# Gated recurrence and ELU MLP on one core: the weights' range check moved to ScalarE and GpSimd, and the schedule of the units rewritten

## Chip, core and metric

The kernel runs on one core of a Trainium2 chip. The metric is the device time of one execution in microseconds (us). TensorE is called PE in the profile, VectorE DVE, ScalarE ACT, GpSimd POOL and SyncE SP.

## What is computed

Attention first: for each batch and head a complex state S of 48 x 48 decays by a per-step, per-channel factor whose magnitude is capped at 0.999, and takes in the outer product of k and v; the output is q times the real part of S. Then an MLP on all 3072 tokens, in float32, with weights that arrive as float64.

```
mag = sqrt(a_re*a_re + a_im*a_im);  scale = minimum(mag, 0.999) / (mag + 1e-6)
for t in range(768):                       # B=4, H=8, D=48
    S_re, S_im = ar*S_re - ai*S_im + k_t v_t^T,  ar*S_im + ai*S_re
    y[t] = q_t . S_re
x = y as (3072, 384)
h = x @ w_in                               # 384 x 2048
g = where(h > 0, h, exp(min(h, 0)) - 1)    # ELU
out = g @ w_out                            # 2048 x 384
```

## The kernel before

The work is cut into 12 **units**: a unit `u` is 128 tokens of two batches (`NB`), all heads. For each unit the kernel makes, in this order:

- *decays*: `squares`, `logarithms`, `noted` (minimum and maximum for a final check that picks a general kernel where the inputs are out of range), `angles` (arc tangent) and `carried` (adds the angle of the unit before on one row). Squares, logarithms and exponentials are ScalarE's (L604 to L618), the products with them GpSimd's (L606, L619, L620; VectorE's for unit 0, by `products`), and two steps are VectorE's: L621, which ends the tangent's argument, and L626, which caps the logarithm.
- *gates*: `turns` (TensorE L664 sums the angles over tokens, VectorE takes the fraction), `waves` (sine and cosine), `decays` (L686, L691), `gated` (q and k times decay and wave: L717, L719, VectorE for q, GpSimd for k).
- *values*, for each batch n: `transposed` q and k (L739, copies L740), `scores` (L747, mask L752), `states` (L768; the state S is added on VectorE, L779, and decayed on GpSimd, L780), `values` (L790, L797, copies L805, L809). `seam` moves some rows of x by DMA from GpSimd (L819).
- *hidden layer*, eight steps `hidden`: six matmul instructions each (L831, twelve records, since a float32 matmul leaves two), then the ELU: ScalarE L836 and L837, VectorE L838 into the tile g.
- *output layer*, eight steps `project`, four instructions each (L847), four steps for each of two blocks of 128 tokens; the result is copied by ScalarE (L853) and stored from SP (L855).

`hidden` and `project` share three PSUM tiles (tag "mlp"), everything else on TensorE shares three (tag "w").

**The weights** come as 14 parts, six of `w_in` (1024 columns) and eight of `w_out` (768 columns), fetched by SP as pairs of 32-bit words (`fetch`) and turned into float32 by `rounded`, seven VectorE operations each, L567 to L585: five build the value from exponent, mantissa and the low word, and the last two (L582, L585) put a value of too small an exponent to zero. `fetches(n)` fetches the next n parts, `converts(n)` issues the next n operations.

**The order** is written out by hand and no scheduler changes it: `plan` is a list of slots, 16 for a unit, each a list of calls, and each engine executes its instructions in the order in which the calls issue them. In the steady part, for unit u, in slots of its own period: `hidden` at 4 to 11, its `project` at 28 to 35, one period later; the gates of unit u + 1 at 0 to 3 and its values from 6; the decays of unit u + 2 at 8 to 12 (`early`). Unit 0 runs ahead of the loop, by itself.

Of the kernel before, what the change touches and what calls it, by code (L numbers as in the profile page):

```python
# [436 lines left out]
def kernel(  # L437
# [94 lines left out]
    def weights_of(kind, m):  # L532

        if kind == "in":
            i, f = m % NI, m // NI * WC
            dst = w_in[:, i, f : f + WC]
            t = sb.tile([C, WC, 2], U32, tag="g", bufs=4, name="w64")
# [20 lines left out]
    def rounded(kind, m):  # L558

        w, dst = raw.pop((kind, m))
# [5 lines left out]
            out=p, in0=hi, scalar1=LOW, scalar2=3, op0=ALU.bitwise_and,  # L568
# [3 lines left out]
            out=f, in0=hi, scalar=TOP, in1=p, op0=ALU.bitwise_and, op1=ALU.bitwise_or  # L572
        )
        yield nc.vector.tensor_scalar(
# [18 lines left out]
    def products(u):  # L593

        return nc.vector if u == 0 else nc.gpsimd
# [12 lines left out]
    def logarithms(u):  # L608
# [11 lines left out]
        products(u).tensor_tensor(out=x0, in0=ai, in1=x0, op=ALU.mult)  # L620
        nc.vector.scalar_tensor_tensor(  # L621
            out=flat(x0), in0=flat(lr), scalar=-2.0, in1=flat(x0), op0=ALU.add, op1=ALU.mult
        )
        x["t"] = x0
        x["l"] = new("n", 6)
        nc.vector.scalar_tensor_tensor(  # L626
            out=flat(x["l"]), in0=flat(lm), scalar=2 * float(np.log(CAP)), in1=flat(e),
            op0=ALU.min, op1=ALU.subtract,
        )

# [271 lines left out]
    SLOTS = 16  # L902

    def recurrence(first, base, n_only=None):
        at = [[0, 1, 2, 3, 5], [3, 4, 6, 7, 8]]
        fns = [
            [
                lambda u, n=n: transposed(u, "q", n), lambda u, n=n: transposed(u, "k", n),
                lambda u, n=n: scores(u, n), lambda u, n=n: states(u, n),
                lambda u, n=n: values(u, n),  # L910
            ]
            for n in range(NB)
        ]
# [3 lines left out]
    def decaying(*at):
        return list(zip(at, (squares, logarithms, noted, angles, carried)))

    def gating(*at):  # L920
        return list(zip(at, (turns, waves, decays, gated)))

    once = recurrence(decaying(0, 1, 1, 3, 3) + gating(4, 5, 5, 6), 7)
    steady = recurrence(gating(0, 1, 2, 3), 6)
    early = decaying(8, 9, 9, 12, 12)


    plan = [[] for _ in range((NU + 3) * SLOTS)]

    def put(at, fn, u):  # L930
        plan[at].append(lambda: fn(u))

    for u in range(1, NU):
        for at, fn in once if u < 3 else steady:
            put((u - 1) * SLOTS + at, fn, u)
        if u > 2:
            for at, fn in early:
                put((u - 2) * SLOTS + at + 2 * (u == 3), fn, u)
# [73 lines left out]
```

## Time and profile before

| | us |
|---|---|
| median of 3 executions | 859.19 (857.25 to 861.69) |
| the profiled execution | 860.39 |
| its span in the profile | 858.6 |
| PE, matmuls: busy | 721.1 (84%) |
| PE, weight loads: busy | 529.8 (62%) |
| VectorE, ScalarE, GpSimd: busy | 327.6, 388.2, 235.3 |

A busy share is a mean over a start, in which the weights are converted, and a steady part, in which unit follows unit; each is to be read from its own stretch. PEclk is the granted clock of TensorE as a share of 2.4 GHz. A row of the timeline has the start in us, the duration in us, and in brackets how long the engine was idle before it and what ended that. Instructions behind one another on an engine may overlap a little, so that a sum of durations is slightly above the time they take.

### The profile page before, as it was taken

Reading aid. Unit: us, or ns where it says so; the run is one execution under the profiler, and the core shown is the slowest. Engines: PE = TensorE matmul, PEld = TensorE weight load, DVE = VectorE, ACT = ScalarE, POOL = GpSimd, SP = SyncE. Lnnn points to the kernel's source line nnn. Section 1 sums busy time; section 2 is a strip of 40 time slices with the busy share of each in tenths; the row PEclk is TensorE's granted clock in tenths of the full one; section 3 lists DMA queues with packets and bytes.
Section 4 is the critical chain, followed back from the end, with each engine's and each line's share of the span. In section 5 each row is a group of like instructions: output and inputs, shape, how many; then the busy total and the mean of one; then the engine's idle time right before and its main releaser. Section 6 shows DMA issues by size and latency. Waiting matters only on the chain.

```text
span 858.6 us, 12795 instructions
## 1 busy us (share of the span) xinstructions
PE 721.1 (84%) x5346; PEld 529.8 (62%) x5346; DVE 327.6 (38%) x401; ACT 388.2 (45%) x591; POOL 235.3 (27%) x210
## 2 busy tenths in 40 slices
PE   1436283559978998999999999999999989999997
PEld 0325072437667686686686686685785776776853
DVE  4973999861323234223323223323323232320200
ACT  5315432544467446346365463472572573431400
POOL 0131132231443242342432523422432421401000
PEclk9667586778989999999999999999999999999999
DMA  9993325501230322122122212302403300000000
GB/s 171 149 170 60 74 52 147 120 1 39 51 66 10 61 47 37 35 47 37 33 48 37 55 26 40 72 7 43 75 2 67 50 2 15 11 1 24 1 21 21
DMA packets 136075, 43.48 MB, mean 51 GB/s; under 512 B 128536, under 2 KB 133192, under 8 KB 135240
## 3 DMA queue, kind: packets, MB, share of 16 engines
q1 hardware_dynamic: 132160, 41.14, 25.5%
q0 software_dynamic: 3776, 1.36, 1.4%
q8 instruction: 44, 0.72, 0.4%
q14 instruction: 23, 0.19, 0.1%
q10 hardware_dynamic: 72, 0.07, 0.0%
HBM read 36.55 MB, written 4.79 MB: 48 GB/s over the span
## 4 chain that ended last, share of the span: by engine, by line
PE 58%; issue 16%; DVE 10%; POOL 8%; ACT 4%; DMA 2%; SPq 1%; DVEq 0%; POOLq 0%; ACTq 0%
PE mlp L847 29%; PE mlp L831 18%; PE w L739 3%; PE w L768 2%; POOL n L619 2%; POOL n L620 2%; DMA w<-in_moe_w_in_dram 2%; PE y L797 2%; PE w L747 2%; PE w L664 1%; DVE g L838 1%; DVE least L634 1%; POOL S L780 1%; DVE most L637 1%; PE w L686 1%
## 5 line engine op out<-in xcount | busy, mean ns | idle before, releaser
L831 PE MATMUL mlp<-x,w_in 128*128 128x256 f32 x1152 | 273.8, 392 | 23.3 <-DMA x<-y 23.2
L847 PE MATMUL mlp<-w_out,g 128*128 128x384 f32 x768 | 271.3, 507 | 16.9 <-DVE g L838 16.9
L831 PEld LDWEIGHTS mlp<-x,w_in 128*128 128x128 f32 x1152 | 221.7, 197 | 58.1 <-issue 25.0
L847 PEld LDWEIGHTS mlp<-w_out,g 128*128 128x128 f32 x768 | 148.6, 197 | 117.8 <-DVE g L838 18.0
L838 DVE SCALAR_TENSOR_TENSOR g<-ee,mlp 128x512 f32<-128x512 f32 x96 | 65.0, 685 | 214.6 <-ACT ee L837 211.7
L836 ACT ACTIVATE ee<-mlp 128x512 f32<-128x512 f32 x96 | 57.1, 595 | 157.0 <-PE mlp L831 124.6
L780 POOL TENSOR_TENSOR S<-S,T 96x384 f32<-96x384 f32 x40 | 35.5, 888 | 206.8 <-DVE S L779 206.8
L853 ACT COPY o<-mlp 128x384 f32<-128x384 f32 x24 | 11.5, 479 | 130.5 <-PE mlp L847 124.5
L739 PE MATMUL w<-ident,qg 128*96 128x128 f32 x192 | 31.0, 303 | 42.0 <-DVE qg L719 36.5
L837 ACT ACTIVATE ee<-ee 128x512 f32<-128x512 f32 x96 | 60.5, 630 | 3.0
L739 PEld LDWEIGHTS w<-ident,qg 128*96 128x96 f32 x192 | 22.5, 138 | 49.0 <-DVE qg L719 39.1
L719 POOL TENSOR_TENSOR kg<-k,cs 128x1536 f32<-128x1536 f32 x11 | 51.9, 4718 | 0.9
L805 ACT COPY x<-y 128x384 f32<-128x384 f32 x24 | 11.3, 473 | 89.5 <-PE y L797 89.5
L740 ACT COPY qt<-w 96x512 f32<-96x512 f32 x48 | 26.8, 579 | 45.2 <-PE w L739 45.0
L621 DVE SCALAR_TENSOR_TENSOR n<-n 128x768 f32<-128x768 f32 x12 | 11.5, 958 | 91.4 <-POOL n L620 91.4
L664 PE MATMUL w<-n,sum_turns 128*128 128x384 f32 x48 | 21.8, 586 | 27.0 <-ACT n L647 21.0
L717 POOL TENSOR_TENSOR k<-k,n 128x768 f32<-128x768 f32 x11 | 23.9, 2171 | 71.7 <-ACT n L691 71.7
L819 POOL DMA_DIRECT2D x<-y x72 | 35.5, 500 | 26.7 <-ACT y L809 26.7
L669 DVE TENSOR_SCALAR rnd<-w 128x384 f32<-128x384 f32 x24 | 13.4, 557 | 73.7 <-PE w L664 72.4
L606 POOL TENSOR_TENSOR n<-n 128x768 f32<-128x768 f32 x11 | 19.9, 1810 | 77.9 <-ACT n L605 77.9
L768 PEld LDWEIGHTS w<-vn,kg 64*96 64x96 f32 x704 | 34.5, 161 | 9.5 <-issue 9.3
L619 POOL TENSOR_TENSOR n<-ar,n 128x768 f32<-128x768 f32 x11 | 20.1, 1824 | 63.8 <-ACT n L617 63.8
(72 smaller groups left out, 791.9 us busy)
## 6 DMA issues: line engine op xcount, KB each, us to landing
w<-in_moe_w_out_dram SPq DMA_DIRECT2D x8, 768.0 KB
ar<-in_a_re_dram SPq DMA_DIRECT2D x24, 192.0 KB, 3.0
ai<-in_a_im_dram SPq DMA_DIRECT2D x24, 192.0 KB, 4.5
w<-in_moe_w_in_dram SPq DMA_DIRECT2D x12, 384.0 KB, 14.3
q<-in_q_dram SPq DMA_DIRECT2D x24, 192.0 KB, 3.5
k<-in_k_dram SPq DMA_DIRECT2D x24, 192.0 KB, 4.8
vn<-in_v_dram SPq DMA_DIRECT2D x24, 192.0 KB, 3.4
out_dram<-o SPq DMA_DIRECT2D x24, 192.0 KB, 2.0
```

Source lines behind the costliest of these rows:

```text
L619: products(u).tensor_tensor(out=lr, in0=ar, in1=x0, op=ALU.mult)
L664: nc.tensor.matmul(t, lhsT=sum_turns, rhs=x["th"][:, n].rearrange("p h d -> p (h d)"), start=True, stop=True,)
L719: eng.tensor_tensor(out=o, in0=g.rearrange("p n h d -> p (n h) d").unsqueeze(2).to_broadcast(shape), in1=x["cs"], op=ALU.mult,)
L739: nc.tensor.transpose(t[:, h], x[key + "g"][:, n, h0 + h], ident)
L768: nc.tensor.matmul(g[:, h], lhsT=x["kg"][ts(c, L), n, h], rhs=vn[u % 2][ts(c, L), n, h, 0:D], start=True, stop=True,)
L780: nc.gpsimd.tensor_tensor(out=new_s, in0=new_s, in1=wide, op=ALU.mult)
L819: nc.gpsimd.dma_start(out=x["x"][ds(j * HP + D, G), i], in_=x["y"][ds(j * HP + i * G, G)])
L831: nc.tensor.matmul(t[:, e], lhsT=w_in[:, i, ts(f + e, C)], rhs=x["x"][:, i], start=(i == 0), stop=(i == NI - 1),)
L836: nc.scalar.activation(out=e, in_=t, func=AF.Relu, scale=-1.0)
L837: nc.scalar.activation(out=e, in_=e, func=AF.Exp, scale=-1.0)
L838: nc.vector.scalar_tensor_tensor(out=x["g", f // 8][:, f % 8 : f % 8 + 2], in0=e, scalar=-1.0, in1=t, op0=ALU.add, op1=ALU.max)
L847: nc.tensor.matmul(x["o"], lhsT=x["g", f // 8][:, f % 8, ts(n, C)], rhs=w_out[:, f], start=(f == 0), stop=(f == NF - 1),)
```

## The change

Four things change. In `rounded`, the two last operations on VectorE go: the high words are squared by ScalarE as float32 (in place), GpSimd compares the square with 2^-30 and multiplies the converted weights in place; the buffer of the fetched words is now read by GpSimd last. `slopes` holds the two VectorE steps that stood in `logarithms`, and is called later. `products` gives VectorE the products of units 0 and 1. And the plan is written anew: the output layer of a unit follows its hidden layer, decays start three slots later, units 0 and 1 run interleaved ahead of the first hidden layer, thirty matmuls on the identity (`warm`) stand ahead of unit 0's transposes, and fetches and conversions have their own tables.

```diff
     def rounded(kind, m):
         yield nc.vector.tensor_scalar(
-            out=p, in0=hi, scalar1=LOW, scalar2=3, op0=ALU.bitwise_and,
+            out=f, in0=hi, scalar1=LOW, scalar2=3, op0=ALU.bitwise_and,
             op1=ALU.logical_shift_left,
         )
...
+        size = hi.bitcast(FP32)
+        nc.scalar.activation(out=size, in_=size, func=AF.Square)
...
-        yield nc.vector.tensor_tensor(out=p, in0=p, in1=f, op=ALU.add)
-        yield nc.vector.tensor_scalar(
-            out=hi, in0=hi, scalar1=EXP, scalar2=None, op0=ALU.bitwise_and
-        )
-        yield nc.vector.scalar_tensor_tensor(
-            out=dst, in0=hi, scalar=float(LEAST), in1=p, op0=ALU.is_ge, op1=ALU.mult
-        )
+        yield nc.vector.tensor_tensor(out=dst, in0=p, in1=f, op=ALU.add)
+        yield nc.gpsimd.tensor_scalar(
+            out=size, in0=size, scalar1=LEAST_SQ, scalar2=None, op0=ALU.is_ge
+        )
+        nc.gpsimd.tensor_tensor(out=dst, in0=dst, in1=size, op=ALU.mult)
...
-        return nc.vector if u == 0 else nc.gpsimd
+        return nc.vector if u < 2 else nc.gpsimd
...
+    def slopes(u):
         nc.vector.scalar_tensor_tensor(
-            out=flat(x0), in0=flat(lr), scalar=-2.0, in1=flat(x0), op0=ALU.add, op1=ALU.mult
+            out=flat(t), in0=flat(w), scalar=-2.0, in1=flat(t), op0=ALU.add, op1=ALU.mult
...
+    def warm(n):
+        t = ps.tile([C, C], FP32, tag="mlp", bufs=3, name="mlp")
+        for _ in range(n):
+            nc.tensor.matmul(t, lhsT=ident, rhs=ident, start=True, stop=True)
...
+    FETCHES = [(-32, 1), (-29, 1), (-27, 1), (-26, 1), (-18, 1), (-12, 1), (-10, 2), (-1.5, 1), (0.5, 1)]
+    FETCHES += [(3.5, 1), (5.5, 1), (7.5, 1), (9.5, 1)]
+    CONVERTS = [(-28, 2), (-26, 2), (-25, 2), (-24, 1)] + [(-20 + i, 1) for i in range(12)]
+    CONVERTS += [(-8 + i, 3) for i in range(22)]
...
+    decays_of(0, -30, -29, -28, -27, -28, -28)
+    gates_of(0, -26, -25, -25, -23)
+    put(-24, warm, 30)
+    values_of(0, -20)
+    decays_of(1, -22, -21, -18.5, -8, -18, -18)
+    gates_of(1, -17, -16, -15.5, -12.5)
+    values_of(1, -10)
+    layer_of(0, 4, 20)
+    layer_of(1, 12, 28)
+    for u in range(2, NU):
+        r = (u - 2) * SLOTS
...
+        decays_of(u, r + 11, r + 12, r + 14, r + 14, r + 15, r + 15)
+        gates_of(u, r + 16, r + 17, r + 18, r + 19)
+        values_of(u, r + 22)
+        layer_of(u, r + 36, r + 44)
```

In it `decays_of` takes the slots of squares, logarithms, slopes, noted, angles and carried, `gates_of` those of turns, waves, decays and gated, `values_of` the first slot of the values, and `layer_of` the first slot of the hidden and of the output layer. `(-8, 3)` in CONVERTS stands for three operations in slot -8.

**VectorE, one steady unit.** Before (g is the ELU's output, a the masked scores, S the state, n the decay tiles, ar and ai the factors):

```order
L838 SCALAR_TENSOR_TENSOR g<-ee,mlp 128x512 x4
L752 TENSOR_TENSOR a<-w,mask 128x512
L838 SCALAR_TENSOR_TENSOR g<-ee,mlp 128x512
L779 TENSOR_TENSOR S<-w,S 96x384 x2
L621 SCALAR_TENSOR_TENSOR n<-n 128x768
L626 SCALAR_TENSOR_TENSOR n<-n 128x768
L634 TENSOR_REDUCE least<-ar 128x1
L637 TENSOR_REDUCE most<-ai 128x1
L838 SCALAR_TENSOR_TENSOR g<-ee,mlp 128x512 x3
L752 TENSOR_TENSOR a<-w,mask 128x512
L653 SCALAR_TENSOR_TENSOR n<-carry,n 1x768
L779 TENSOR_TENSOR S<-w,S 96x384 x2
```

Now:

```order
L845 SCALAR_TENSOR_TENSOR g<-ee,mlp 128x512 x5
L759 TENSOR_TENSOR a<-w,mask 128x512
L845 SCALAR_TENSOR_TENSOR g<-ee,mlp 128x512
L786 TENSOR_TENSOR S<-w,S 96x384 x2
L845 SCALAR_TENSOR_TENSOR g<-ee,mlp 128x512 x2
L759 TENSOR_TENSOR a<-w,mask 128x512
L786 TENSOR_TENSOR S<-w,S 96x384 x2
L629 SCALAR_TENSOR_TENSOR n<-n 128x768
L632 SCALAR_TENSOR_TENSOR n<-n 128x768
L641 TENSOR_REDUCE least<-ar 128x1
L644 TENSOR_REDUCE most<-ai 128x1
L660 SCALAR_TENSOR_TENSOR n<-carry,n 1x768
```

The four decay operations moved from ahead of the last three ELU steps to behind all eight and behind both state sums.

**ScalarE, the end of the same unit's hidden layer.** Before (the last rows of the ELU, then the arc tangent with its table, then the copies of y and of the output tile o):

```order
L837 ACTIVATE ee<-ee 128x512
L647 ACT_TABLE_LOAD
L647 ACTIVATE n<-n 128x768
L805 COPY x<-y 128x2x3x64
L809 COPY y<-y 128x128
L853 COPY o<-mlp 128x384
```

Now:

```order
L620 ACT_TABLE_LOAD
L620 ACTIVATE n<-n 128x768
L621 ACTIVATE n<-n,ln_eps 128x768
L812 COPY x<-y 128x2x3x64
L816 COPY y<-y 128x128
L860 COPY o<-mlp 128x384
L654 ACT_TABLE_LOAD
L654 ACTIVATE n<-n 128x768
```

The arc tangent stands behind the copy of o now, and the logarithms and exponentials (L620, L621) stand right ahead of the copies of y.

**VectorE, the first ELU steps of unit 0.** Before, between operations of the weights (w, wp, wf, w_in):

```order
L578 SCALAR_TENSOR_TENSOR wp<-w_127,wp 128x1024
L838 SCALAR_TENSOR_TENSOR g<-ee,mlp 128x512
L581 TENSOR_TENSOR wp<-wp,wf 128x1024
L582 TENSOR_SCALAR w_127<-w_127 128x1024
L585 SCALAR_TENSOR_TENSOR w_in<-w_127,wp 128x1024
```

Now:

```order
L583 SCALAR_TENSOR_TENSOR wp<-w_758,wp 128x768
L586 TENSOR_TENSOR w_out<-wp,wf 128x768
L570 TENSOR_SCALAR wf<-w_782 128x768
L845 SCALAR_TENSOR_TENSOR g<-ee,mlp 128x512
L574 SCALAR_TENSOR_TENSOR wf<-w_782,wf 128x768
L579 TENSOR_SCALAR wp<-wf 128x768
L583 SCALAR_TENSOR_TENSOR wp<-w_782,wp 128x768
L845 SCALAR_TENSOR_TENSOR g<-ee,mlp 128x512
L586 TENSOR_TENSOR w_out<-wp,wf 128x768
```

The first ELU step stood in the fourth weight part and stands in the tenth now; the last addition of the weights stands between the second and the third ELU step of unit 1. On GpSimd each part's compare and multiply (L587, L590) follow the order of the parts, and those of the last two stand around the products of unit 2's decays.

## Rows read from the trace of the kernel before

**Rows 1.** Windows: start and end, length, busy (instructions) of PE, PEld, DVE, ACT, POOL; PEclk, DMA, GB/s.

```profile
0.00:34.30 34.30, 5.12 (x8) 2.15 (x8) 20.59 (x23) 17.51 (x20) 3.17 (x11) 0.86 1.00 160
34.30:57.60 23.30, 14.70 (x256) 12.78 (x256) 22.71 (x25) 7.24 (x14) 7.56 (x10) 0.72 1.13 164
```

**Rows 2.** Windows: one unit of the steady part.

```profile
428.58:490.13 61.55, 58.97 (x458) 43.37 (x457) 19.57 (x25) 31.89 (x49) 21.07 (x19) 0.97 0.22 41
```

**Rows 3.** Timeline of all engines in that unit, around the last ELU steps.

```profile
457.24 0.96 DVE L621 SCALAR_TENSOR_TENSOR n<-n 128x768 f32<-128x768 f32 x1 [8.70 <-POOL n L620]
...
460.70 1.27 DVE L838 SCALAR_TENSOR_TENSOR g<-ee,mlp 128x512 f32<-128x512 f32 x2
...
461.44 4.51 PE L847 MATMUL mlp<-w_out,g 128*128 128x384 f32 x8 [2.11 <-DVE g L838]
```

**Rows 4.** Windows: behind a short stop, and behind the 2.11 us stop.

```profile
123.40:124.10 0.70, 0.01 (x1) 0.00 (x0) 0.70 (x3) 0.00 (x0) 0.00 (x0) 1.00 0.00 0
124.10:124.90 0.80, 0.64 (x4) 0.39 (x4) 0.80 (x3) 0.05 (x1) 0.00 (x0) 1.00 0.00 0
...
461.40:463.00 1.60, 1.56 (x3) 0.96 (x4) 0.81 (x2) 1.48 (x3) 0.00 (x0) 0.50 1.09 216
```

**Rows 5.** Timeline of VectorE: the two kinds of weight operations, at both widths.

```profile
94.78 0.69 DVE L567 TENSOR_SCALAR wp<-w 128x1024 uint32<-128x1024 uint32 x1
95.50 1.23 DVE L571 SCALAR_TENSOR_TENSOR wf<-w,wp 128x1024 uint32<-128x1024 uint32 x1
...
134.58 0.55 DVE L567 TENSOR_SCALAR wp<-w 128x768 uint32<-128x768 uint32 x1
135.16 0.96 DVE L571 SCALAR_TENSOR_TENSOR wf<-w,wp 128x768 uint32<-128x768 uint32 x1
```

**Rows 6.** Groups by line and shape: busy us, mean ns | idle before.

```profile
L847 PE MATMUL mlp<-w_out,g 128*128 128x384 f32 x768 | 271.3, 507 | 16.9 <-DVE g L838 16.9
L838 DVE SCALAR_TENSOR_TENSOR g<-ee,mlp 128x512 f32<-128x512 f32 x96 | 65.0, 685 | 214.6 <-ACT ee L837 211.7 <-PE w L686 3.0
...
L606 POOL TENSOR_TENSOR n<-n 128x768 f32<-128x768 f32 x11 | 19.9, 1810 | 77.9 <-ACT n L605 77.9
...
L604 ACT ACTIVATE n<-ar 128x768 f32<-128x768 f32 x12 | 10.0, 835 | 0.0
...
L882 POOL MEMSET vn<- 128x256 f32 x2 | 0.6, 311 | 0.0
```

**Rows 7.** Timeline of all engines: a weight operation beside GpSimd's product.

```profile
107.10 4.85 POOL L719 TENSOR_TENSOR kg<-k,cs 128x1536 f32<-128x1536 f32 x1
108.56 4.21 DVE L571 SCALAR_TENSOR_TENSOR wf<-w,wp 128x768 uint32<-128x768 uint32 x1
```

**Rows 8.** Timeline of the steady unit: decay chain and TensorE's groups.

```profile
449.67 0.84 ACT L614 ACTIVATE n<-n 128x768 f32<-128x768 f32 x1
...
455.39 1.81 POOL L620 TENSOR_TENSOR n<-ai,n 128x768 f32<-128x768 f32 x1
...
462.75 1.28 ACT L647 ACT_TABLE_LOAD   x1
...
464.92 0.94 DVE L653 SCALAR_TENSOR_TENSOR n<-carry,n 1x768 f32<-1x768 f32 x1 [0.87 <-ACT n L647]
465.88 1.44 PEld L768 LDWEIGHTS w<-vn,kg 64*96 64x96 f32 x32 [0.55 <-issue]
...
467.37 2.85 PE L847 MATMUL mlp<-w_out,g 128*128 128x384 f32 x8
...
470.15 0.69 PE L790 MATMUL y<-a,vn 64*64 64x64 f32 x32
...
471.80 1.56 PE L847 MATMUL mlp<-w_out,g 128*128 128x384 f32 x4
```

**Rows 9.** Chain that ended last, its end: start us, us, what.

```profile
789.91 20.72 PE mlp L831 x96
...
823.65 28.59 PE mlp L847 x88
```

More of the change, by code (lines that the diff above doesn't have):

```diff
@@ L917, in decaying @@
[L917 to L938, printed above, removed]
@@ new lines, with put, decays_of @@
+    FETCHES = [(-32, 1), (-29, 1), (-27, 1), (-26, 1), (-18, 1), (-12, 1), (-10, 2), (-1.5, 1), (0.5, 1)]
+    FETCHES += [(3.5, 1), (5.5, 1), (7.5, 1), (9.5, 1)]
+    CONVERTS = [(-28, 2), (-26, 2), (-25, 2), (-24, 1)] + [(-20 + i, 1) for i in range(12)]
+    CONVERTS += [(-8 + i, 3) for i in range(22)]
+    SLOTS = 16
+    plan = []
+    def put(at, fn, *args):
+        plan.append((at, len(plan), lambda: fn(*args)))
+    def decays_of(u, *at):
+        for x, fn in zip(at, (squares, logarithms, slopes, noted, angles, carried)):
+            put(x, fn, u)
@@ new lines, in gates_of, with values_of, layer_of @@
+    def gates_of(u, *at):
+        for x, fn in zip(at, (turns, waves, decays, gated)):
+            put(x, fn, u)
+    def values_of(u, base):
+        for n, at in enumerate([[0, 1, 2, 3, 5], [3, 4, 6, 7, 8]]):
+            for x, (fn, *args) in zip(at, (
+                (transposed, u, "q", n), (transposed, u, "k", n), (scores, u, n),
+                (states, u, n), (values, u, n),
+            )):
+                put(base + x, fn, *args)
+        put(base + 9, seam, u)
+    def layer_of(u, at_h, at_p):
+        for m in range(NF // 2):
+            put(at_h + m, hidden, u, 2 * m)
@@ L948 @@
         for m in range(NF // 2):
             n, q4 = divmod(m, NF // 4)
-            put(
-                (u + 1) * SLOTS + (9 if u == 0 else 12) + m,
-                lambda u, n=n, q4=q4: project(u, n, 4 * q4, 4 * q4 + 4), u,
-            )
-    fetches(1)
-    load_qk(0)
-    fetches(1)
-    load_v(0)
-    fetches(1)
-    load_a(1)
-    fetches(1)
-    between = {angles: 3, decays: 4, gated: 4}
-    for at, fn in once:
-        fn(0)
-        if fn is gated:
-            load_qk(1)
-        converts(between.get(fn, int(at >= 7)))
@@ L968 @@
-    load_v(1)
-    for at, fns in enumerate(plan):
-        if at < 2 * SLOTS:
-            fetches(1 if at < 8 else at % 2)
-            converts(3 if at < 8 else 4 if at < SLOTS else 3)
-        for fn in fns:
-            fn()
-        if at == NU * SLOTS:
-            verdict()
+            put(at_p + m, project, u, n, 4 * q4, 4 * q4 + 4)
+    for at, fn, u in (
+        (-31, load_qk, 0), (-30, load_v, 0), (-28, load_a, 1), (-21, load_qk, 1), (-20, load_v, 1),
+    ):
+        put(at, fn, u)
@@ L977 @@
+    for at, n in FETCHES:
+        put(at, fetches, n)
+    for at, n in CONVERTS:
+        put(at, converts, n)
+    put(NU * SLOTS, verdict)
+    for _, _, do in sorted(plan, key=lambda x: x[:2]):
+        do()
     ctx.close()
```

44 lines of the change are left out of this document (15 added, 29 removed).

## The prediction

> **What bounds the kernel now.** I read the stretches of the span first, then the chain of waits, then the timeline of one unit of work on all engines. In the steady part one unit takes 61.55 us, of which TensorE is busy 58.97 [rows 2]. So TensorE sets the time there, and only its stops can be won. The reader finds one such stop in each unit: VectorE starts a decay step at 457.24 after 8.70 us of waiting for GpSimd, the ELU steps (L838) queued behind it start only at 460.70, and TensorE, whose PSUM tile for the next output group they free, waits 2.11 us [rows 3]. That wait costs more than itself: right behind it the granted clock is 0.50 (1.2 GHz) where it was 1.00 (2.4 GHz) before; behind a stop of 0.7 us, from 123.40 to 124.10, it stayed at 1.00 [rows 4]. The eight matmuls that began at 461.44 took 4.51 us including the slow stretch [rows 3], where eight at full clock move on in 2.78 (467.37 to 470.15 [rows 8]). That is 1.7 us, and with the remainder of the slow stretch I take 1.84. So a stop is worth 2.11 + 1.84 = 3.95 us, and a unit without it takes 61.55 - 3.95 = 57.6 us.
>
> Ahead of the steady part the bound is another one. VectorE is busy 20.59 of the first 34.3 us and 22.71 of the next 23.3 [rows 1]: it converts the weights, and nothing of the MLP can run without them.
>
> **The change, part by part.**
>
> *Decay steps behind the ELU steps.* The 3.95 us stop goes. The trace has it in eight units (TensorE's matmuls of L847 wait 16.9 us in all for L838 [rows 6], eight times 2.11), which makes -31.6 us. But the whole decay chain now starts three slots later, and two things become late. I count from the end of a unit's last hidden matmul.
>
> First, GpSimd's queue holds the two products of the decays (L619, L620 before, L622, L623 now) ahead of the state product S. S must wait for: the y matmuls 1.65 us (470.15 to 471.80 [rows 8]), ScalarE's two copies of them, an estimated 0.7 from their 384 and 128 columns at the squares' rate, two squares and GpSimd's add, 2 x 0.835 + 1.81 = 3.5 [rows 6], logarithms and products 7.53 (449.67 to 457.20 [rows 8]), and S's own multiply, 0.9 at 384 columns: some 14.3 us. TensorE arrives where it needs S after 1.65 + 2.78 + 1.1 + 2.78 + 1.49 + 2.78 + 0.6 = 13.2 us: output-layer groups as from 467.37 to 470.15, the state matmuls 465.88 to 467.37 [rows 8], a part of the y matmuls, an estimated 0.6 of the 1.65, and for the scores an estimate of 1.1 from these like groups of 32 small matmuls. So a wait of about 1.1 us.
>
> Second, the arc tangent now stands on ScalarE behind the copy of the output tile, which ends only when TensorE has finished the first token half. The copy of 384 columns, an estimated 0.5 at the squares' rate [rows 6], then table load, arc tangent and VectorE's carry step (462.75 to 465.86, 3.1 us [rows 8]) make 3.7 us with gaps; TensorE has one group of eight matmuls, 2.6 us, to do before it needs the angles. Again about 1.1 us. Neither wait is in the trace of before; their bounds are 0 (the chains run a little faster than I add up) and 2.11 each with the clock's fall. I take 1.1 without a fall, because they are nearer to the 0.7 us stop that left the clock at 1.00 than to the 2.11 us one [rows 4]. Nine units have late decays: 9 x 2.15 = +19.4 us. The net of this part is -12.2 us.
>
> *Output layer right behind the first.* It moves 64 matmul records of each unit one unit earlier and adds or removes none: 0 us, as long as their cover holds. What they covered was TensorE's time under gates and values; the new neighbours there are the same unit's matmuls, so the cover stays.
>
> *Weights' range check.* VectorE loses two operations in each of 14 weight parts: 0.69 + 1.23 us in six parts of 1024 columns, 0.55 + 0.96 in eight of 768 [rows 5], in all 23.6 us. ScalarE gets a square each (0.84 us at 768 columns [rows 6]), which hides beside VectorE's next operations. GpSimd gets a multiply, 1.81 us at 768 columns [rows 6] and so 2.41 at 1024, and a compare that the trace does not show. Its bounds are GpSimd's memset, 311 ns for 256 columns [rows 6], hence 0.93 and 1.24 us, and the multiply's own price. I take the lower, as the compare reads one operand and not two. That is 6 x 3.65 + 8 x 2.74 = 44 us on GpSimd (58 at the upper bound). The Trainium skill, GPSIMD Engine Reference, section 4.1, calls one-input work on this engine roughly line rate; 1024 columns would be an estimated 0.85 us, and the sum some 3 us lower.
>
> Is GpSimd's 44 us beside VectorE's work? The rows say mostly not. VectorE's L571, 0.96 us alone [rows 5], took 4.21 us when it met GpSimd's product of 4.85 us and ended 0.8 us after it [rows 7]: operations with two SBUF inputs waited it out. VectorE's operations on PSUM (L838, the masks, the states) and its own waits leave room; they are about a third of its time in this stretch. So I put two thirds, 29 us, on VectorE's path; bounds 0 and 44.
>
> *First units reordered, unit 1's products on VectorE, fetches.* I add up VectorE's queue up to the last addition of the weights, which now stands between the second and third ELU of the second unit. The first 57.6 us hold 43.30 us of VectorE work [rows 1], of which three weight parts of seven operations (3 x 6.99) and 5.0 of a fourth; so unit 0's own work is 17.4, and unit 1's the same, because its products are now VectorE's. Weights: five operations stay, 2 x 0.69 + 3 x 1.23 = 5.07 and 2 x 0.55 + 3 x 0.96 = 3.98 [rows 5], together 62.3. Ten ELU steps at 0.685 [rows 6]: 6.9. Work: 34.8 + 62.3 + 6.9 = 104. Waits: 57.6 - 43.3 = 14.3 in the first unit with the 7.8 us start; for unit 1, whose logarithms stand uncovered, 3.9 (the 7.53 of [rows 8] less two products of 1.81) and, an estimate, as much again for its sines, together 8. With GpSimd's 29 the last addition ends near 104 + 22.3 + 29 = 155 us. Then the four decay operations (457.24 to 460.70, 3.5 us [rows 3]), a carry step of 0.94 [rows 8] and two hidden steps of 20.72 / 8 us [rows 9] pass until the second unit's hidden layer ends: **165 us**.
>
> What queues behind the new waits: on SP, the fetch of a weight part now waits for GpSimd's multiply of the part whose buffer it takes, and behind it stand the loads of unit 2; these are needed some 30 us later, so I cost them at nothing. If that cover went, one late load of two tensors, 786 KB at 160 GB/s [rows 1], would cost 5 us.
>
> *Filler matmuls.* Thirty of 128 columns, sixty records of half a hidden matmul's columns: 20.72 / 96 / 2 = 0.11 us each at full clock, twice that at half, so 6.5 to 13 us. They stand between decays and transposes of unit 0, where TensorE has some 10 us free. Cost 0 to 3, gain 0 to 3 (faster transposes, whose copies wait for ScalarE's logarithms anyway): 0.
>
> **The sum.** From 165 us on TensorE does ten units at 57.6 = 576, the output layers of units 0 and 1 at 28.59 x 64 / 88 = 20.8 each [rows 9] = 41.6, the new waits 19.4, and the tail behind the last matmul, 858.6 - 852.2 = 6.4 [rows 9]: 643.4. The span becomes 808, the execution 808 + 1.8 = 810 against 860.39; that execution stands 1.2 us above the median of 859.19, so the forecast is **809 us**.
>
> **The rivals.**
> 1. *GpSimd's checks run free beside VectorE.* For it: many of VectorE's steps in that stretch read PSUM. Against: rows 7. Then 29 us go: 780.
> 2. *They exclude each other wholly.* For it: the 4.21 us row. Against: the room just named. All 44 us on the path: 824. The Trainium skill, Advanced Engine Details and Errata, section VectorE Performance Modes, says that GpSimd instructions and two-port VectorE instructions block each other; by that rule, taken for every operation here, this is the case, and the row of 4.21 us agrees.
> 3. *The two new waits let the clock fall* as the 2.11 us one did: 18 x 1.84 = +33 us: 842. For it: the fall at 461.40; against: none behind 0.7 us.
> 4. *The new waits aren't there*, because ScalarE and GpSimd run a little ahead of my count: 790.
> 5. *Slower than before.* GpSimd's compare is the price: the 14 compares stand in VectorE's way one by one, and each microsecond more costs 14. The forecast has 50 us to lose, so it decides at some 3.6 us more than I took, a compare near 5 us, twice GpSimd's two-operand rate. At 6 us: 809 + 14 x 4.7 = 875. Against: no row of GpSimd is so slow per column.
> 6. *The change doesn't do what it says*, and the ELU steps still wait for GpSimd: 809 + 31.6 = 841.
>
> **How the numbers follow.** The forecast has 0.40; rivals 1 and 2 0.18 and 0.13; 3 and 6 0.12 and 0.02; 4 0.07; 5 0.08, of which 0.02 within the bound that follows. The range runs from 776 (rival 1 with the cheaper end of the small costs) to 842 (rival 3). About 0.5% is what a measurement of this kernel can tell from no change. Faster: 0.92; the same: 0.02; slower: 0.06.
>
> **What would show it.** Right: the decay step L629 (L621 before) starts behind the last ELU step, and TensorE's wait for the ELU steps is gone; a steady unit near 59.7 us; the hidden layer of the second unit ending near 165 us; VectorE operations stretched where GpSimd's multiply or compare runs. Wrong: a steady unit of 57.6 (rival 4) or 63 (rival 3); hidden layers ending near 136 (rival 1) or 180 (rival 2); GpSimd busy without pause up to 200 us (rival 5).

## The result and the profile after

The changed kernel takes **831.63 us** (median of 4 runs, 829.47 to 831.91) against 858.22 us (854.53 to 861.69) for the kernel before, run beside it: ratio 0.9685, 95% interval 0.964 to 0.973. The profiled span is 829.6 us, its mean granted clock 0.952. The forecast was 809 us in a range of 776 to 842: the direction and the range held, and of the 50 us forecast 27 came.

Windows of the changed kernel, columns as in [rows 1]: up to the end of the last weight addition, from there to the end of unit 1's hidden layer, and one steady unit:

```profile
0.00:165.20 165.20, 90.43 (x736) 73.10 (x737) 132.82 (x123) 79.61 (x109) 94.83 (x60) 0.78 0.63 116
165.20:184.75 19.55, 14.69 (x54) 11.19 (x53) 10.32 (x13) 11.12 (x14) 2.41 (x2) 0.83 0.42 61
247.52:307.53 60.01, 57.67 (x457) 42.54 (x456) 19.76 (x26) 32.21 (x49) 22.50 (x19) 1.00 0.25 42
```

Its steady unit is 60.01 us where the forecast had 59.7 and [rows 2] 61.55. From 184.75 us to the end it takes 644.85 us, forecast 643.4. So all that is missing was lost ahead of 184.75 us, which the forecast had put at 165. Of the 29.0 us between the two profiled spans (858.6 and 829.6), nine steady units account for some 14 (1.54 us each); the rest was won outside them, and no run takes apart which piece of the new order won it. TensorE's timeline of the steady unit, the only rows there with a wait of half a microsecond or more, shows what it lost:

```profile
289.57 0.99 PE L804 MATMUL y<-qt,S 96*48 96x64 f32 x28 [0.65 <-POOL S L787]
...
297.13 1.53 PE L671 MATMUL w<-n,sum_turns 128*128 128x384 f32 x4 [1.21 <-DVE n L660]
```

The stop for the ELU in [rows 3] is gone, and on VectorE the first decay step stands behind the last ELU step:

```profile
276.82 0.69 DVE L845 SCALAR_TENSOR_TENSOR g<-ee,mlp 128x512 f32<-128x512 f32 x1 [2.78 <-ACT ee L844]
...
290.03 0.94 DVE L629 SCALAR_TENSOR_TENSOR n<-n 128x768 f32<-128x768 f32 x1
```

The two forecast waits, for the state product and for the carry step, are there, at 0.65 and 1.21 us, and the granted clock of the unit is 1.00 throughout: no fall behind either.

The groups of the weight conversion in the changed kernel, VectorE's for parts of 768 and 1024 columns (L570, L574, L579, L583, L586; [rows 5] has 0.55 and 0.96, 0.69 and 1.23 us for the two kinds), then ScalarE's square (L578), GpSimd's compare (L587) and multiply (L590):

```profile
L574 DVE SCALAR_TENSOR_TENSOR wf<-w,wf 128x768 uint32<-128x768 uint32 x8 | 14.1, 1766 | 0.1
L574 DVE SCALAR_TENSOR_TENSOR wf<-w,wf 128x1024 uint32<-128x1024 uint32 x6 | 11.2, 1870 | 0.1
...
L570 DVE TENSOR_SCALAR wf<-w 128x768 uint32<-128x768 uint32 x8 | 8.4, 1055 | 0.3
...
L587 POOL TENSOR_SCALAR w<-w 128x768 f32<-128x768 f32 x8 | 20.3, 2539 | 6.2 <-ACT w L578 5.7
L587 POOL TENSOR_SCALAR w<-w 128x1024 f32<-128x1024 f32 x6 | 20.0, 3338 | 0.6
...
L590 POOL TENSOR_TENSOR w_out<-w_out,w 128x768 f32<-128x768 f32 x8 | 16.7, 2094 | 1.9 <-DVE w_out L586 1.6
L590 POOL TENSOR_TENSOR w_in<-w_in,w 128x1024 f32<-128x1024 f32 x6 | 15.4, 2575 | 0.5
...
L578 ACT ACTIVATE w<-w 128x768 f32<-128x768 f32 x8 | 7.4, 920 | 34.1 <-DVE wf L574 34.1
```

GpSimd spends 72.4 us on the check, not 44: the compare, 2.54 and 3.34 us, is dearer than the multiply with its two operands. VectorE's L574 takes 1.8 and 1.5 times its own time. And in the eight parts of 768 columns the square waits 34.1 us for VectorE, with ELU operations behind it on ScalarE.

The section on the change leaves one thing out: the buffers are shared in another way. In the kernel before, the fetched `w_out` parts had a tag of their own. Now half of them have the tag `g1`, which the ELU's tiles of odd units use too, and GpSimd's multiply is the last to read a fetched part. So VectorE's first ELU step of unit 1 waits for GpSimd and starts as the multiply ends (157.45):

```profile
153.13 2.41 POOL L587 TENSOR_SCALAR w<-w 128x768 f32<-128x768 f32 x1
...
155.62 1.83 POOL L590 TENSOR_TENSOR w_out<-w_out,w 128x768 f32<-128x768 f32 x1
...
157.48 0.69 DVE L845 SCALAR_TENSOR_TENSOR g<-ee,mlp 128x512 f32<-128x512 f32 x1 [4.02 <-POOL w_out L590]
```

VectorE is idle from 153.46 on, so the first two rows also show GpSimd's two operations with next to nothing beside them.

Two theories could explain the 20 us lost in the start. **A:** GpSimd's operations stretch VectorE's, and that is the price. **B:** the square, waiting in ScalarE's queue ahead of the ELU, makes TensorE wait. Beside both stands a third possibility, that the forecast of the start was wrong without any check.

### The profile page after: what moved, and what is told of

Its sections match the earlier page's. It is cut to its first block, busy times and chain, and to the rows that moved or that the text cites. A ratio compares the mean times of both kernels' runs of the same rounds, so it can differ in the third digit from the quotient of the medians.

```text
span 829.6 us, 12975 instructions
## 1 busy us (share of the span) xinstructions
PE 720.4 (87%) x5406; PEld 532.3 (64%) x5406; DVE 336.2 (41%) x378; ACT 403.0 (49%) x604; POOL 307.4 (37%) x233
## 4 chain that ended last, share of the span: by engine, by line
PE 49%; issue 18%; DVE 12%; ACT 8%; POOL 7%; DMA 3%; SPq 2%; POOLq 0%; ACTq 0%; DVEq 0%
PE mlp L838 21%; PE mlp L854 17%; PE w L746 3%; POOL S L787 3%; PE w L671 2%; DVE wf L574 2%; POOL n L623 2%; POOL n L622 2%; DMA w<-in_moe_w_out_dram 2%; PE w L754 2%; DMA w<-in_moe_w_in_dram 2%; SPq L509 1%; PE w L693 1%; ACT L654 1%; DVE wp L583 1%
## 5 line engine op out<-in xcount | busy, mean ns | idle before, releaser
L838 PE MATMUL mlp<-x,w_in 128*128 128x256 f32 x1152 | 268.0, 388 | 24.3 <-DVE g L845 24.3
L854 PE MATMUL mlp<-w_out,g 128*128 128x384 f32 x768 | 262.9, 492 | 0.0
L854 PEld LDWEIGHTS mlp<-w_out,g 128*128 128x128 f32 x768 | 142.2, 190 | 92.0
L787 POOL TENSOR_TENSOR S<-S,T 96x384 f32<-96x384 f32 x40 | 48.2, 1206 | 191.2 <-DVE S L786 191.2
L786 DVE TENSOR_TENSOR S<-w,S 96x384 f32<-96x384 f32 x40 | 22.1, 552 | 77.0 <-PE w L775 39.2
L726 POOL TENSOR_TENSOR kg<-k,cs 128x1536 f32<-128x1536 f32 x10 | 47.1, 4713 | 0.8
L775 PEld LDWEIGHTS w<-vn,kg 64*96 64x96 f32 x704 | 37.1, 171 | 12.0 <-issue 9.0
L747 ACT COPY qt<-w 96x512 f32<-96x512 f32 x48 | 26.4, 577 | 35.9 <-PE w L746 35.7
L587 POOL TENSOR_SCALAR w<-w 128x768 f32<-128x768 f32 (+1 forms) x14 | 40.3, 2881 | 6.7 <-ACT w L578 5.7
L775 PE MATMUL w<-vn,kg 64*96 64x48 f32 x704 | 40.3, 257 | 2.5 <-ACT n L698 1.7
L578 ACT ACTIVATE w<-w 128x768 f32<-128x768 f32 (+1 forms) x14 | 14.3, 1019 | 51.9 <-DVE wf L574 38.5
```

Of the source, the lines that this page charges most:

```text
L587: yield nc.gpsimd.tensor_scalar(out=size, in0=size, scalar1=LEAST_SQ, scalar2=None, op0=ALU.is_ge)
L726: eng.tensor_tensor(out=o, in0=g.rearrange("p n h d -> p (n h) d").unsqueeze(2).to_broadcast(shape), in1=x["cs"], op=ALU.mult,)
L747: nc.scalar.copy(out=o[:, h0 : h0 + 4], in_=t)
L775: nc.tensor.matmul(g[:, h], lhsT=x["kg"][ts(c, L), n, h], rhs=vn[u % 2][ts(c, L), n, h, 0:D], start=True, stop=True,)
L787: nc.gpsimd.tensor_tensor(out=new_s, in0=new_s, in1=wide, op=ALU.mult)
L838: nc.tensor.matmul(t[:, e], lhsT=w_in[:, i, ts(f + e, C)], rhs=x["x"][:, i], start=(i == 0), stop=(i == NI - 1),)
```

## Experiments on the range check

**The check back on VectorE.** The rest of the change as it is:

```diff
-        nc.scalar.activation(out=size, in_=size, func=AF.Square)
...
-        yield nc.vector.tensor_tensor(out=dst, in0=p, in1=f, op=ALU.add)
-        yield nc.gpsimd.tensor_scalar(
-            out=size, in0=size, scalar1=LEAST_SQ, scalar2=None, op0=ALU.is_ge
-        )
-        nc.gpsimd.tensor_tensor(out=dst, in0=dst, in1=size, op=ALU.mult)
+        yield nc.vector.tensor_tensor(out=p, in0=p, in1=f, op=ALU.add)
+        yield nc.vector.tensor_scalar(
+            out=hi, in0=hi, scalar1=EXP, scalar2=None, op0=ALU.bitwise_and
+        )
+        nc.vector.scalar_tensor_tensor(
+            out=dst, in0=hi, scalar=float(LEAST), in1=p, op0=ALU.is_ge, op1=ALU.mult
+        )
```

Expected: 

> The changed kernel with the range check as it was: two operations on VectorE in each weight part, none on ScalarE and GpSimd. Theory A (the checks on GpSimd stretch VectorE's weight operations, 93.5 us in the profile against 62.3 uncontended, and hold up the ELU steps): VectorE gets 23.6 us back to do and loses 31 us of stretching and some 4 us of waiting, so about 820 us, faster than the changed kernel's 831.6. Rival B (the move relieves VectorE): 831.6 + 23.6 = 855 us.

Measured 816.99 us (816.24 to 818.38), ratio 0.9539 (0.9507 to 0.9571), near the 820 of A and far from the 855 of B. In this schedule, moving the check off VectorE costs 14.6 us.

**Only the check moved.** The kernel before, with `rounded` as changed and nothing else (the square counts as a step of its own here, so that a part keeps its seven steps in the old plan):

```diff
...
+        yield nc.scalar.activation(out=size, in_=size, func=AF.Square)
...
-        yield nc.vector.tensor_scalar(
-            out=hi, in0=hi, scalar1=EXP, scalar2=None, op0=ALU.bitwise_and
-        )
-        nc.vector.scalar_tensor_tensor(
-            out=dst, in0=hi, scalar=float(LEAST), in1=p, op0=ALU.is_ge, op1=ALU.mult
-        )
+        yield nc.gpsimd.tensor_scalar(
+            out=size, in0=size, scalar1=LEAST_SQ, scalar2=None, op0=ALU.is_ge
+        )
+        nc.gpsimd.tensor_tensor(out=dst, in0=dst, in1=size, op=ALU.mult)
```

Expected: 

> The kernel before with nothing but the range check moved to ScalarE and GpSimd. Theory A: 23.6 us less and about 31 us more on VectorE's path, so no gain: 860 to 870 us against 858. Rival B: 858 - 23.6 = 835 us.

Measured 870.77 us, ratio 1.0168 (1.0134 to 1.0203), just above A's 860 to 870. In the old program the move costs 12.6 us against the 858.15 us of the kernel before, run beside it. The new order brings the gain; this part of the change gives some of it back.

**No check.** The changed kernel with all three operations taken out:

```diff
-        nc.scalar.activation(out=size, in_=size, func=AF.Square)
...
-        yield nc.gpsimd.tensor_scalar(
-            out=size, in0=size, scalar1=LEAST_SQ, scalar2=None, op0=ALU.is_ge
-        )
-        nc.gpsimd.tensor_tensor(out=dst, in0=dst, in1=size, op=ALU.mult)
+        yield True
```

Expected: 

> The changed kernel without the range check: no square, compare or multiply, five VectorE operations a part (small weights are not put to zero). Theory A: the stretching of 31 us and the waits at the ELU steps go, 790 to 797 us. Rival B (GpSimd's work is hidden beside VectorE): 828 to 832 us. It also tells what the check costs in this schedule at most.

Measured 801.58 us, ratio 0.9348 (0.9315 to 0.938): faster, as A said, but less so than its 790 to 797. So the whole check costs 30.0 us on the new path, and as VectorE's own two operations 15.4.

**Which of the three operations.** Three kernels keep one or two of them:

```diff
 square_only:
-        yield nc.gpsimd.tensor_scalar(out=size, ..., op0=ALU.is_ge)
-        nc.gpsimd.tensor_tensor(out=dst, in0=dst, in1=size, op=ALU.mult)
+        yield True
 square_and_compare:
-        nc.gpsimd.tensor_tensor(out=dst, in0=dst, in1=size, op=ALU.mult)
 square_and_multiply:
-        yield nc.gpsimd.tensor_scalar(out=size, ..., op0=ALU.is_ge)
+        yield True
```

Expected: 

> The changed kernel with ScalarE's square left in, and GpSimd's compare and multiply taken out: the range check is computed in part and never applied. no_check (801.58 us) is the same without the square; the changed kernel (831.63 us) is the same with all three. Theory A (GpSimd's two operations cost the 30 us: the multiply keeps VectorE's operations out and the compare is long): 802 to 807, VectorE's weight operations at their short durations. Rival B (the square costs them, by its place in ScalarE's queue: it waits for VectorE's second weight operation, and the ELU's operations wait behind it): 815 to 828, with TensorE waiting in each part of the first hidden layers.

> The changed kernel with GpSimd's multiply of the weights taken out, square and compare left in: the range check is not applied. With square_only it divides the 30 us. Theory A1 (the multiply is the cost, since it and VectorE's operations with two inputs exclude each other): 804 to 812, VectorE's second weight operation back near 1.0 to 1.3 us. Theory A2 (the compare is, with its 2.5 to 3.3 us each, 40 us in all): 818 to 828, and VectorE's operations beside a compare are still stretched. Rival B as for square_only: within 4 us of square_only, and that above 815.

> The changed kernel with GpSimd's compare taken out; the weights are multiplied by the square itself, so the outputs are others, at the same work. square_only is 804.69 us, square_and_compare 812.08, all three 831.63. Theory A (the multiply is the price by itself, since it shuts VectorE's operations with two SBUF inputs out): 820 to 826, about 19 us over square_only, VectorE's second weight operation at 1.7 us or more. Rival B (it is the sum: compare and multiply together make GpSimd the engine that comes last; either one alone costs some 7 us): 808 to 814.

Measured, with VectorE's windows from 0 to the end of the last weight operation (busy; the rest is idle) and the start of the first output layer:

| kernel | us | ratio to before (95%) | last weight operation ends | VectorE busy | idle | output layer starts |
|---|---|---|---|---|---|---|
| no_check | 801.58 | 0.9348 (0.9315–0.938) | 137.13 | 104.47 | 32.7 | 154.73 |
| square_only | 804.69 | 0.9368 (0.9334–0.9402) | 139.70 | 104.51 | 35.2 | 157.39 |
| square_and_compare | 812.08 | 0.9463 (0.9427–0.9499) | 147.82 | 115.89 | 31.9 | 165.64 |
| square_and_multiply | 821.73 | 0.9574 (0.9541–0.9607) | 155.15 | 119.47 | 35.7 | 174.07 |
| changed kernel | 831.63 | 0.9685 (0.964–0.973) | 165.15 | 132.77 | 32.4 | 184.75 |
| check_on_vector | 816.99 | 0.9539 (0.9507–0.9571) | 150.86 | 127.41 | 23.5 | 169.90 |

By these times the square costs 3.1 us, the compare 7.4 and the multiply 17.0; the three add up to 27.5 of 30.0. The medians of the kernel before, run beside them, lie up to 1.3 us apart (858.07 to 859.38), and the ratio intervals of no_check and square_only overlap, so the square's 3.1 us are less sure than the other two; the profiles show its last weight operation 2.6 us later. Theory A holds for the price of the check and B falls: the square's waits for VectorE are long but hold up little that counts. Neither explains the 20 us that were missing, since the forecast had a price of 29 us for the check in it: these come from the third possibility (below). Of A's two forms A1 is nearer, as the multiply is the larger price, but the compare has one of its own (812.08, at the upper end of A1). The table also shows how A works. VectorE's idle time stays within 4 us in the first five rows (the 4.02 us wait for GpSimd above stands in the fifth, where no_check has no wait at that ELU step and 1.70 us for ScalarE at the next); its *busy* time grows, by 11.4 us with the compare, 15.0 with the multiply and 28.3 with both, and the end moves with it, by 8.12, 15.45 and 25.45 us from square_only. When VectorE does the check itself, its busy time grows by 22.9 us but 9.2 of them fall into idle time, and the end moves by only 13.7.

The same place of two of these kernels, VectorE and GpSimd. With the compare alone (L574 and L586 have two SBUF inputs):

```profile
127.94 2.63 POOL L587 TENSOR_SCALAR w<-w 128x768 f32<-128x768 f32 x1 [3.14 <-ACT w L578]
...
129.62 0.95 DVE L586 TENSOR_TENSOR w_out<-wp,wf 128x768 f32<-128x768 f32 x1
...
131.68 0.95 DVE L574 SCALAR_TENSOR_TENSOR wf<-w,wf 128x768 uint32<-128x768 uint32 x1
```

With the multiply alone:

```profile
130.12 2.17 POOL L588 TENSOR_TENSOR w_out<-w_out,w 128x768 f32<-128x768 f32 x1 [4.69 <-DVE w_out L586]
...
131.10 2.01 DVE L574 SCALAR_TENSOR_TENSOR wf<-w,wf 128x768 uint32<-128x768 uint32 x1
```

L586 starts 1.68 us into a compare and takes its 0.95 us all the same; L574 stands behind the compare there and takes 0.95. With the multiply, L574 starts 0.98 us into it and ends 0.82 us after the multiply's end (133.11 against 132.29), as the product of [rows 7] made it do. But the compare isn't free everywhere: in square_and_compare, earlier in the start, it met L574 like this:

```profile
82.22 3.28 POOL L587 TENSOR_SCALAR w<-w 128x1024 f32<-128x1024 f32 x1
82.72 2.04 DVE L574 SCALAR_TENSOR_TENSOR wf<-w,wf 128x1024 uint32<-128x1024 uint32 x1
```

L574 is stretched to 2.04 us here and still ends 0.74 us ahead of the compare. Per microsecond of GpSimd the compare stretches VectorE by 0.27 (11.4 of 42.1 us) and the multiply by 0.46 (15.0 of 32.3).

**Square on ScalarE, the rest as one VectorE operation**, with the earlier decays of the next section:

```diff
-        yield nc.vector.tensor_tensor(out=dst, in0=p, in1=f, op=ALU.add)
...
-        nc.gpsimd.tensor_tensor(out=dst, in0=dst, in1=size, op=ALU.mult)
+        yield nc.vector.tensor_tensor(out=p, in0=p, in1=f, op=ALU.add)
+        yield nc.vector.scalar_tensor_tensor(
+            out=dst, in0=size, scalar=LEAST_SQ, in1=p, op0=ALU.is_ge, op1=ALU.mult
+        )
...
-        decays_of(u, r + 11, r + 12, r + 14, r + 14, r + 15, r + 15)
+        decays_of(u, r + 8, r + 9, r + 12, r + 12, r + 13, r + 13)
```

Expected: 

> vector_check_decays_earlier (794.28 us) with the check's first operation as ScalarE's square and only the second, a compare and multiply in one instruction, on VectorE. VectorE loses 0.55 or 0.69 us in 14 parts, 8.5 us. The check's two operations cost 816.99 - 801.58 = 15.4 us for 23.6 us of VectorE's time, so 8.5 us are worth 5.6, and the square costs 3.1 (square_only less no_check). Theory A: 794.3 - 5.6 + 3.1 = 791.8. Rival B (the square's wait for VectorE, with the ELU behind it on ScalarE, costs more once VectorE is fuller than in square_only): 794.3 or more.

Measured 794.95 us (793.32 to 796.09, 6 runs), ratio 0.9262 (0.9237 to 0.9288), where the two-operation form (below) has 794.28 (793.16 to 794.68), ratio 0.9247. The 2.5 us forecast for it didn't come, and the time is the one that rival B gave; the two kernels can't be told apart. Its output layer starts at 168.96 us, that of the two-operation form at 167.55. Whether the square's wait is the reason, as B has it, isn't shown.

## Experiments on the order

**Decays three slots earlier, slopes still behind all eight ELU steps:**

```diff
-        decays_of(u, r + 11, r + 12, r + 14, r + 14, r + 15, r + 15)
+        decays_of(u, r + 8, r + 9, r + 12, r + 12, r + 13, r + 13)
```

Expected: 

> The changed kernel with squares, logarithms and angles at slots 8, 9 and 13 of the unit in place of 11, 12 and 15; the two decay steps of VectorE stay behind the last ELU step (slot 12 in place of 14). Theory A (the waits of 0.65 and 1.22 us in each steady unit come from the late chain): nine units lose 1.87 us each, 831.6 - 17 = 815 us, a steady unit of about 58.1 us. Rival C (logarithms ahead of the last ELU steps on ScalarE hold those up instead): no gain, 830 us or more.

Measured 809.15 us (808.35 to 809.64), ratio 0.9444 (0.9413 to 0.9475), 6 us below A's 815. Its steady unit has neither wait, and is the 57.6 us that the forecast took for a unit without stops:

```profile
243.27:300.97 57.70, 57.23 (x457) 42.55 (x457) 19.68 (x26) 31.88 (x49) 21.72 (x19) 1.00 0.27 44
```

Nine units gain 2.31 us each, 20.8 together, and the start another 2.0 (its output layer begins at 182.72). So the late decays cost what I had priced, 19.4 us, and a bit more; and the old stop doesn't come back when they go.

**Slopes in front of the last ELU steps again.** First two of them:

```diff
-        decays_of(u, r + 11, r + 12, r + 14, r + 14, r + 15, r + 15)
+        decays_of(u, r + 8, r + 9, r + 9, r + 9, r + 12, r + 12)
```

Expected: 

> The changed kernel with the decay preparation pulled ahead as in decays_earlier, but with VectorE's four slope and reduction operations (3.7 us) in front of the last ELU operations of a unit again, as in the kernel before. Everything else is decays_earlier (809.15 us). Theory A (VectorE's in-order queue makes the wait: an ELU operation that stands behind the slopes waits for them and for the turns in front of them, and TensorE waits for the ELU): TensorE's wait of about 2 us for an ELU operation comes back in each of nine units, with a clock fall behind it, and the unit is 61 to 61.6 us as in the kernel before, so 809 + 9 x 3.5 = 840 (835 to 845). Rival B (TensorE's wait in the kernel before came of the turns being issued late, whatever their place among the ELU operations): the unit stays near 57.7 us and the time at 809 to 813.

Measured 815.46 us, ratio 0.9497 (0.9463 to 0.9531): B by the unit, though the time is above its 809 to 813. VectorE's timeline there reads as in [rows 3], the slope L629 behind 8.70 us of waiting and the two ELU operations 3.5 us behind it:

```profile
281.22 0.96 DVE L629 SCALAR_TENSOR_TENSOR n<-n 128x768 f32<-128x768 f32 x1 [8.70 <-POOL n L623]
...
284.69 1.27 DVE L845 SCALAR_TENSOR_TENSOR g<-ee,mlp 128x512 f32<-128x512 f32 x2
```

but TensorE waits for neither of them (its longest wait in the unit is 0.47 us, for a state sum), and the unit is 57.70 us (297.20 to 354.90 from one turns step to the next). The 6.3 us above decays_earlier lie mostly in the start, where the output layer begins 5.3 us later (187.97).

Then one hidden part further ahead, so that three ELU operations stand behind the slopes as in the kernel before:

```diff
-        decays_of(u, r + 11, r + 12, r + 14, r + 14, r + 15, r + 15)
+        decays_of(u, r + 7.5, r + 8.5, r + 8.5, r + 8.5, r + 11.5, r + 11.5)
```

Expected: 

> slopes_early once more, with VectorE's slopes one hidden part further ahead: three ELU operations of a unit stand behind them, as in the kernel before, where slopes_early (815.46 us) left two behind them and its trace shows those two ELU operations as late as in the kernel before, but no wait of TensorE. Theory A (what TensorE waits for is the PSUM tile that the first ELU operation behind the slopes frees; three tiles are in turn, so two late ELU operations are covered and the third is not): a wait near 2.1 us in front of the output layer's matmuls in each steady unit, the unit 60 to 61.6 us, the time 815.5 + 8 x (2.1 to 3.95) = 832 to 847. Rival B (the output layer behind the first, or the other order, leaves slack for a third one too): no wait, the unit at 57.7, 809 to 816.

Measured 854.42 us, ratio 0.996 (0.994 to 0.998), the unit 62.93 us. Neither theory foresaw what stops TensorE there, on ScalarE's and TensorE's timeline:

```profile
330.94 0.92 ACT L621 ACTIVATE n<-n,ln_eps 128x768 f32<-128x768 f32 x1
331.76 0.57 ACT L843 ACTIVATE ee<-mlp 128x512 f32<-128x512 f32 x1
332.37 0.63 ACT L844 ACTIVATE ee<-ee 128x512 f32<-128x512 f32 x1
332.91 0.56 ACT L747 COPY qt<-w 96x512 f32<-96x512 f32 x1
333.52 1.09 PE L746 MATMUL w<-ident,qg 128*96 128x128 f32 x4 [3.00 <-ACT qt L747]
334.40 5.05 PE L838 MATMUL mlp<-x,w_in 128*128 128x256 f32 x12
```

The half slot moved the logarithms on ScalarE as well, in front of an ELU step and the copies of q; TensorE waits 3.00 us for a copy, and the next twelve hidden matmuls take 5.05 us where the same group takes 2.75 to 2.86 at full clock. The granted clock from 334.40 to 337.00 is 0.50 (1.2 GHz). The difference of 62.93 to 57.70 is the wait, 2.5 us longer than the 0.47 us at the same place of slopes_early, the transposes behind it (1.09 us for 0.64) and 2.3 us in the hidden matmuls. So the kernel moved two things and doesn't settle the question it was made for: how much of the old stop was the slopes' place alone stays open. What the pair shows is that half a slot decides whether a queue that runs in the order of the program stops TensorE, and that 2.5 us more of a stop cost 5.2.

**Both together:** the check on VectorE and the decays earlier. Expected: 

> check_on_vector and decays_earlier together: the range check as VectorE's two operations as in the kernel before, and the decay preparation three slots earlier. check_on_vector was 14.6 us below the changed kernel, decays_earlier 22.5 us. Theory A (the one acts on the start, the other on nine steady units, so they add): 831.6 - 14.6 - 22.5 = 794.5, range 791 to 799, the steady unit 57.7 us. Rival B (they meet in the start: with VectorE fuller there, unit 2's decay steps pulled ahead displace weight operations): 800 to 810.

Measured **794.28 us** (793.16 to 794.68), ratio 0.9247 (0.9214 to 0.928), with square_one_vector_op the fastest of all that ran. The two gains add to 0.3 us, which is closer than the runs can tell, and the steady unit is 57.70 us again.

**No filler matmuls:**

```diff
-    put(-24, warm, 30)
```

Expected: 

> The changed kernel without the filler matmuls. In its trace they take 22.14 to 29.0 us, TensorE is idle for 6.68 us behind them, and the transposes start slow. Theory A (they do nothing for the time): 831.6 within 2 us. Rival B (they raise TensorE's clock for the transposes and first matmuls of unit 0): 835 to 840.

Measured 831.41 us (829.43 to 832.72), ratio 0.9696 (0.9663 to 0.9729): no difference. In the changed kernel the granted clock is 1.00 while they run, but TensorE stands idle behind them, and the next transposes take 1.94 us at a granted clock of 0.50:

```profile
22.14 6.86 PE L913 MATMUL mlp<-ident 128*128 128x128 f32 x60
35.68 1.94 PE L746 MATMUL w<-ident,qg 128*96 128x128 f32 x8 [6.68 <-DVE qg L726]
```

Without them the same transposes stand at 35.50, and take 1.94 us at 0.50 as well, behind 13.29 us of idleness.

## Why the prediction was right in part

*Decay steps behind the ELU steps: the unit right, its cause not shown.* A unit of 59.7 us was forecast, 60.0 measured; both new waits are where they were put (0.65 and 1.21 us for 1.1 each), without a fall of the clock. Rivals 3 (unit 63), 4 (57.6) and 6 (ELU still waits) fall. The price of the old stop, 3.95 us a unit, is borne out too: without any of these stops the unit is 57.70 us (decays_earlier), 3.85 below the 61.55 of the kernel before. But that the stop went *because* the slopes moved isn't shown. In slopes_early they stand in front of two ELU steps again, and no stop comes back.

*Output layer behind the first: nothing against the 0.* The steady unit has no stop from it. It wasn't undone by itself, so its share isn't shown; after slopes_early it is a candidate for what ended the old stop, as the output layer's matmuls were the ones that waited.

*The range check: the sum right by luck, both factors wrong.* The forecast was 29 us on VectorE's path, as two thirds of 44. Measured are 28.3 us (132.8 less 104.5), as 0.39 of 72.4. The step of this part that failed is "I take the lower, as the compare reads one operand and not two": 0.93 and 1.24 us were taken, 2.54 and 3.34 measured, and even the upper bound, the multiply's 1.81 and 2.41, was too low. The Trainium skill, GPSIMD Engine Reference, section 4.1, calls one-input work there roughly line rate, an estimated 0.85 us for 1024 columns; the 3338 ns of this compare disagree. The other error made up for it: a compare stretches VectorE by 0.27 of its time only. (The multiply alone was priced rightly: 1.83 us at 155.62 for 1.81 forecast; beside VectorE it takes 2.09 on average.) Rival 2, full exclusion, would have put all 72 us on the path. The prediction's own sign for that rival, unit 1's hidden layer ending near 180, came (184.75), but for other reasons, as the table below shows. The rule beside that rival (the Trainium skill, Advanced Engine Details and Errata, VectorE Performance Modes: GpSimd's instructions and VectorE's two-port ones block each other), taken for every operation as there, holds in the rows for the multiply and not for the compare at 127.94, beside which L586 ran its 0.95 us. Rival 5's point of decision, a compare near 5 us, wasn't reached. That the square "hides beside VectorE's next operations" was off by some 3 us.

What the prediction had not worked out is what VectorE gains by losing its two operations: it counts 23.6 us as lost to VectorE, but check_on_vector less no_check is 15.4, because in that start part of them runs in time in which VectorE would wait anyway. By its figures the move would cost 29 - 23.6 = 5.4 us; it costs 14.6. The sum that gave 809 us doesn't use the 23.6, so this isn't part of what it missed.

*First units: wrong, and the main error.* no_check shows the start without any check, so its own terms can be compared:

| term | forecast | measured |
|---|---|---|
| VectorE's work up to the last weight addition | 104 | 104.5 (no_check) |
| its waits up to there | 22.3 | 32.7 (no_check), 32.4 (changed kernel) |
| stretched by GpSimd | 29 | 28.3 |
| last weight addition ends | 155 | 165.15 |
| from there to the end of unit 1's hidden layer | 9.6 | 19.6 |
| the rest | 643.4 | 644.85 |
| span | 808 | 829.6 |

Two terms fail, by 10 us each. "For unit 1 ... together 8" us of waits: VectorE's rows in no_check that waited longest behind unit 1's logarithms, with the causes the forecast left out, are

```profile
51.08 0.56 DVE L671 TENSOR_SCALAR rnd<-w 128x384 f32<-128x384 f32 x1 [2.73 <-PE w L666]
...
57.73 0.69 DVE L754 TENSOR_TENSOR a<-w,mask 128x512 f32<-128x512 f32 x1 [2.36 <-PE w L749]
...
63.18 0.55 DVE L779 TENSOR_TENSOR S<-w,T 96x384 f32<-96x384 f32 x1 [3.63 <-PE w L770]
```

each a wait for TensorE, 8.7 us, where the forecast had 4 for ScalarE's sines. Another 1.70 us is for an ELU step, 1.0 lies in unit 0, and some 3 us are waits below half a microsecond, which I hadn't counted at all. Why TensorE came late at these three places wasn't followed up.

And the **end term**: TensorE's timeline of the changed kernel behind the last addition:

```profile
172.06 2.92 PE L671 MATMUL w<-n,sum_turns 128*128 128x384 f32 x4 [4.86 <-DVE n L660]
...
174.78 6.26 PE L838 MATMUL mlp<-x,w_in 128*128 128x256 f32 x24
...
180.87 1.45 PE L693 MATMUL w<-n,sum_logs 128*128 128x384 f32 x4
...
182.16 2.75 PE L838 MATMUL mlp<-x,w_in 128*128 128x256 f32 x12
```

VectorE's carry step ends 6.9 us behind the last addition instead of 4.4: I had left out the two ELU steps (0.67 each) that stand among the decay operations, and the last multiply stretches L629 to 2.28 us. Then TensorE does unit 2's turns and logarithm sums and three hidden groups, 12.7 us, where I had two hidden groups, 5.2; the turns behind the 4.86 us stop take 2.92, twice the 1.45 that the same matmuls take in decays_earlier (172.37), with no stop right in front of them; the granted clock from 172.06 to 174.90 is 0.50.

*Filler matmuls: right at 0* (no_filler: 0.2 us, inside the measurement). The fetches, also put at 0, weren't tried by themselves.

## What to carry to other kernels

Before work is moved off a full engine, ask how much of it runs in time in which that engine would wait anyway (here 8 of 23.6 us), how far the new engine stretches what stays behind (here 28 us), and whether a buffer now comes free later (here a wait of 4.02 us); a kernel without the work tells the first two. A step moved to end one wait should be tried a few slots either way, as it may open others (here 20.8 us of 0.65 and 1.21 us waits and what follows them). And the time behind the last item of a chain is counted by every step that is queued there, on each engine.

## What the runs showed that I had not expected

- GpSimd's compare of every second fp32 word took 2.54 us at 768 and 3.34 at 1024 columns; its multiply of two operands, one with the same stride, 2.09 and 2.58. With VectorE idle beside them they took 2.41 and 1.83 us at 768 columns. So the stride of one input cost the multiply nothing against the 1.81 us of the dense product [rows 6]; whether the stride of input and output together or the compare itself makes the other dear was not tried.
- The compare let VectorE's operation with two SBUF inputs through at 0.95 us in one place and stretched it to 2.04 in another; GpSimd's spans are rough, so where inside its span the compare holds VectorE up stays open.
- 6.86 us of filler matmuls at a granted clock of 1.00 left the transposes, 6.68 us later, at 0.50 and 1.94 us, the same as without them.
